# A fused attention and two-MLP kernel: values of two units issued from SP, zero matmuls in TensorE's pauses, and a new order

## The chip, the cores and the metric

The kernel runs on one core of a Trainium2 chip. The metric is the device time of one execution in microseconds. The core has five instruction streams: TensorE (PE, with its weight loads PEld), VectorE (DVE), ScalarE (ACT), GpSimd (POOL) and SyncE (SP), which here only issues DMAs. ACT issues a few DMAs too, at the start.

## The reference

Three stages follow each other, all in float32.

```python
# attention: 4 batches, 8 heads, 768 positions, 64 wide, 8 memory positions
for c in range(768 // 32):                       # chunks of 32 queries
    # keys and values: 8 memory rows, 16 to the left, the chunk, 8 to the right
    scores = (q_c @ k_full.T) / 8
    a = exp(scores - max(scores)); a = a / (sum(a) + 1e-9)
    out[c] = a @ v_full
x = out as 3072 tokens x 512
# first MLP
h = x @ w_in                                     # 512 -> 2048
P = a0 + a1*h + a2*h**2 + a3*h**3
Q = 1 + |b0|*|h| + |b1|*h**2
x = (P / (Q + 1e-6)) @ w_out                     # 2048 -> 512
# second MLP
y = (((x @ w1) * (x @ w2)) @ w3) @ w_out2        # 512 -> 1024, 1024 -> 512
```

## The kernel before

Attention goes in 24 units of 128 queries (two blocks of 64, all 8 heads). A unit is loaded as one tile of queries and keys (`qk`, 640 KB, L329, two buffers) and three pieces of values (L348: 64, 56 and 8 partitions, 524 KB together). `s_pe` (L370) makes its scores with 64 small matmuls; DVE and ACT do the softmax (L378 to L408: maximum, subtraction, exponent, sum, epsilon, reciprocal, scaling); `t_pe` (L413) transposes the weights into PSUM, `t_copy` (L421) copies them into `aT`, `v_pe` (L428) multiplies by the values, and `v_parts` (L436, L438) splits the result into a high and a low part. Every product that follows is made of three matmuls on such pairs (high by high, high by low, low by high; `mm3`, L317).

Three units make a block of 384 tokens, 8 blocks in all. For each of them and each of 16 slices of the 2048 hidden columns there is a first-layer product (`gemm1`, 36 matmuls in three groups for the first three slices, 12 each; tile `h`), a rational function over it that runs through ACT, POOL and DVE (L453 to L503, tiles `W`, `Q`, `A`, then `gh` and `gl`), and a second-layer product (`gemm2`, 12 matmuls on the four accumulators `acc`). The first eight slices of blocks 0 and 1 come first (`SEG`), so that the weights needed early are few. The second MLP follows with its own products (`ab`, `w3o`, `pr`).

The weights come as 64-bit floats of 512 KB a chunk (L270) into a ring of four raw buffers. `decode` turns a chunk into a high and a low part: ACT scales the upper words (L275), ACT or DVE takes the low bits (L281, L283), DVE joins them in two steps (L288, L290), ACT rounds the high part (L298), and POOL or DVE makes the low part (L301). A raw buffer is free again when the last of these has read it. Sixteen chunks (eight of `w_in`, eight of `w_out`) are needed for the first eight slices.

Every step is an object with a wanted time `t`, engines with costs, steps that it comes after, and ring slots that it takes. `order()` (L137) goes through them as a list scheduler and gives each engine its order; the table `SHIFT` moves single wanted times. The program's order on each engine is then fixed: an instruction waits for what it needs, and all behind it on its engine wait too. DMAs take one of eight completion semaphores in turn, whichever engine issues them, and a DMA waits until the earlier one on its semaphore has landed.

At the start, `start()` clears `aT` on POOL, loads the coefficients and an identity from ACT, and calls `load_v` for the three units of block 0. Those nine DMAs are issued by ACT, all others by SP:

```python
(act if u < UPB else sp).dma_start(out=t[r0:r1], ...)
```

The values of unit 0 lie in a raw buffer, those of unit 1 in the tile `x2_t` (named `x_t` in rows), those of unit 2 and all later ones in the one value buffer.

Of the kernel before, what the change touches and what calls it, by code (L numbers as in the profile page):

```python
# [7 lines left out]
F32 = mybir.dt.float32  # L8
# [8 lines left out]
P = 128  # L17
# [7 lines left out]
NS = 2  # L25
# [12 lines left out]
UPB = N // UQ  # L38
# [20 lines left out]
def attention_rational_mlp_gated_mlp(  # L59
# [33 lines left out]
    x2n = []  # L93

# [42 lines left out]
    def order():  # L137
        LOOK = 0.000
        warm = [0.0]
        todo, held, free, done = {}, {r: {} if rings[r] < 0 else [] for r in rings}, {"dma": 1.9, "act": 2.0}, []  # L140
# [52 lines left out]
        while len(done) < len(steps):  # L193
# [18 lines left out]
            if e == "pe":  # L212
                gap = s - free.get(e, 0.0)
                if gap > (4.0 if warm[0] >= 5.0 else 0.3):
                    warm[0] = 0.0
                if warm[0] < 5.0:
                    slow = min(2 * c, 5.0 - warm[0]) if c > 1 else 2 * c
                    warm[0] += slow if c > 1 else 0.0
                    c += slow / 2
# [117 lines left out]
    def load_v(u):  # L337
        b, j = divmod(u, UPS)
        if u == 0:
            t = raw32("v").rearrange("p (s h d) -> p s h d", s=NS, h=H)  # L340
        elif u == 1:
            t = x2_t.rearrange("p a c n -> p (a c n)")[:, :NS * H * D].rearrange("p (s h d) -> p s h d", s=NS, h=H)
        else:
            t = v_t[u % VBUF]
        vt[u] = t
        for r0, r1, k0 in ((0, CK, 0), (CK, P - NMEM, W1), (P - NMEM, P, 0)):
            if r1 < P or j < VBUF or u < UPB:
                (act if u < UPB else sp).dma_start(out=t[r0:r1], in_=vW[b, j * NS:(j + 1) * NS, k0:k0 + r1 - r0].rearrange("s k h d -> k s h d"))  # L348
# [280 lines left out]
    H0 = -3.298  # L629


    MODES = "nHhhkhNNnNNNHMNHnNhMMmHnnHNNhnMH"
# [4 lines left out]
    def start():  # L637
        pool.memset(aT, 0.0)
        act.preload_act_table_set("natural_log_exp_and_others")
        act.dma_start(out=cf, in_=coef)  # L640
        act.dma_start(out=idn, in_=ident)
        act.activation(out=cf[:, 4:6], in_=cf[:, 4:6], func=AF.Abs)
        act.activation(out=cf[:, 0:4], in_=cf[:, 0:4], func=AF.Copy, scale=-1.0)
        slots[:] = [("raw", 0)]
        for u in range(UPB):
            load_v(u)
# [4 lines left out]
    T0 = -2.290; UP = 0.175; A0 = -1.147; AS = 2.865  # L651
# [7 lines left out]

    SOFT = 3 * UPB  # L660
    VLAND = (7.6, 9.6, 11.6)
    LEAD = 15
    LEAD2 = 4
    A1 = -3.238
    A2 = -11.920

    def loads(u, t):
        lq[u] = step(t - 3, {"dma": 2.4 if u < 2 else 1.95}, lambda: load_qk(u), *old(first, lq[u - 1]), take=("q",))
        vm = u <= UPB or u % UPS < VBUF
        lv[u] = step(t - 2, {"none": VLAND[u]} if u < UPB else {"dma": 2.3}, lambda: u < UPB or load_v(u), *old(first, lv[u - 1] if u >= UPB else None), take=("raw",) if u == 0 else ("x2", "x2") if u == 1 else ("v",))  # L670
# [18 lines left out]
    def attend(u):  # L689
# [4 lines left out]
        tag1, tag2, tag3 = (("acc0", "acc1")[u % 2], ("h", "acc2")[u % 2], "acc3") if blk == 0 else TAGS1 if blk == 1 else ("h",) * 3  # L694
# [20 lines left out]
    R = (2.092,1.123,-0.489,1.317,7.957,11.098,8.651,1.756,-1.609,1.055,0.592,-0.348,-3.832,0.495)  # L715
    DI = 2.568
    DO = -1.081
    WI, WO = {}, {}
    SI = 0.414
    SO = 1.306  # L720
    DJ = -0.936
    DP = -3.866
    SJ = 0.526
# [45 lines left out]
    u = UPB  # L769
# [389 lines left out]
    for x, n in late:  # L1159
        x.after.append(G1[n])  # L1160
    SHIFT = {0: -8, 1: -23.66, 2: 1.74, 3: -13.58, 4: -13.83, 5: -46, 6: -23.07, 7: 3.51, 8: -44.34, 9: -49.07, 10: -32.57,
# [175 lines left out]
```

## Time and profile before

| | us |
|---|---|
| median of 3 runs (1071.61 to 1075.4) | 1072.48 |
| profiled execution | 1071.7 |
| its span, first to last instruction | 1069.9 |
| PE busy | 1034.6 (97%) |
| PEld busy | 982.5 (92%) |
| DVE busy | 737.6 (69%) |
| ACT busy | 664.1 (62%) |
| POOL busy | 505.7 (47%) |

The busy shares are means over the whole span. PE's is near full in all but the first two and the last of the page's 40 slices, while those of DVE, ACT and POOL fall from the first half to the second. The 1.8 us between the span and the profiled execution's time are start and end of the execution. The chain that ended last names PE for 80% of the span, ACT for 8%, DMA for 5%.

### The profile page before, as it was taken

The page shows a single profiled execution, that of the slowest core. Times are in us where ns is not written, and L with a number is a line of the kernel's source. Part 1 is how long each engine was busy: PE and PEld are TensorE (multiplying, and loading weights), DVE is VectorE, ACT ScalarE, POOL GpSimd, SP SyncE. Part 2 cuts the span into 40 slices and gives each one's busy share as a digit, 9 for nine tenths or more (in the row PEclk, how much of TensorE's full clock was granted, in tenths as well). Part 3 has the DMA queues.
Part 4 walks back from the last instruction along what each step waited for, and adds up shares of the span by engine and source line. Part 5 has one row for each costly group of instructions (what it writes and reads, how often), then busy time and mean ns, then how long its engine had stood idle before and what let it go on. Part 6 is the DMA issues. An engine that isn't in the chain of part 4 may idle for free.

```text
span 1069.9 us, 19764 instructions
## 1 busy us (share of the span) xinstructions
PE 1034.6 (97%) x7632; PEld 982.5 (92%) x7632; DVE 737.6 (69%) x1300; ACT 664.1 (62%) x1272; POOL 505.7 (47%) x490
## 2 busy tenths in 40 slices
PE   2699999999999999999999999999999999999998
PEld 2689999999999999999999999988899999998997
DVE  3899999877877767777778887678474653652330
ACT  2798998877676767767768996644342352342222
POOL 1464577644344544444455666543033362344233
PEclk9999999999999999999999999999999999999999
DMA  8755432123411211211131335544523122312101
GB/s 231 253 166 162 140 124 79 57 72 103 118 44 44 74 44 46 74 43 44 49 99 60 119 99 169 164 143 155 177 99 119 53 77 70 111 51 73 66 17 59
DMA packets 59613, 105.61 MB, mean 99 GB/s; under 512 B 4384, under 2 KB 29088, under 8 KB 59520
## 3 DMA queue, kind: packets, MB, share of 16 engines
q1 hardware_dynamic: 58350, 102.71, 30.6%
q10 hardware_dynamic: 1170, 1.64, 0.7%
q8 instruction: 60, 0.98, 0.4%
q14 instruction: 33, 0.27, 0.1%
HBM read 85.99 MB, written 18.35 MB: 98 GB/s over the span
## 4 chain that ended last, share of the span: by engine, by line
PE 80%; ACT 8%; DMA 5%; DVE 3%; issue 2%; POOL 1%; SPq 0%; ACTq 0%; POOLq 0%; DVEq 0%
PE acc L317 32%; PE h L317 21%; PE pr L317 16%; PE w3o L317 4%; PE xo L428 2%; PE sc L370 2%; PE ab L317 1%; ACT Q L462 1%; DMA w<-in_w_out_dram 1%; DMA qk<-in_qkT_dram 1%; DMA w<-in_w_in_dram 1%; ACT A L453 1%; PE at L413 1%; ACT W L453 1%; DMA w<-in_w_dram 1%
## 5 line engine op out<-in xcount | busy, mean ns | idle before, releaser
L317 PE MATMUL acc<-gh,wB 128*128 128x384 f32 x1024 | 283.7, 340 | 0.4 <-POOL wB L301 0.4
L317 PE MATMUL h<-xr,wA 128*128 128x384 f32 x1344 | 253.8, 338 | 0.6 <-DVE A L494 0.6
L317 PEld LDWEIGHTS h<-xr,wA 128*128 128x128 f32 x1344 | 234.9, 189 | 2.6 <-issue 0.8
L468 POOL TENSOR_TENSOR W<-W,Q 128x384 f32<-128x384 f32 x128 | 132.3, 1033 | 122.7 <-ACT Q L462 120.1
L317 PEld LDWEIGHTS acc<-gh,wB 128*128 128x128 f32 x1024 | 186.7, 188 | 2.4 <-POOL wB L301 0.7
L317 PE MATMUL acc<-gl,wB 128*128 128x384 f32 x512 | 172.3, 337 | 0.5 <-POOL gl L503 0.5
L503 POOL TENSOR_TENSOR gl<-A,gh 128x384 fp32r<-128x384 f32 x128 | 132.1, 1032 | 49.9 <-ACT gh L498 42.2
L486 DVE SCALAR_TENSOR_TENSOR A<-A,cf,h 128x384 f32<-128x384 f32 x128 | 78.1, 610 | 58.3 <-ACT h L482 57.8
L317 PE MATMUL pr<-wB,wA 128*128 128x384 f32 x624 | 113.7, 335 | 0.0
L317 PEld LDWEIGHTS pr<-wB,wA 128*128 128x128 f32 x624 | 109.2, 188 | 1.3
L473 DVE TENSOR_TENSOR A<-A,h 128x384 f32<-128x384 f32 x128 | 70.6, 552 | 43.2 <-ACT A L453 40.1
L317 PEld LDWEIGHTS acc<-gl,wB 128*128 128x128 f32 x512 | 96.1, 188 | 0.8 <-POOL gl L503 0.8
L317 PE MATMUL acc<-wB,gh 128*128 128x512 f32 x294 | 92.4, 395 | 0.0
L453 ACT ACTIVATE W<-h 128x384 f32<-128x384 f32 x128 | 62.3, 486 | 47.9 <-PE h L317 47.0
L462 ACT ACTIVATE Q<-W,cf 128x384 f32<-128x384 f32 x118 | 83.7, 709 | 3.8
L453 ACT ACTIVATE A<-h,cf 128x384 f32<-128x384 f32 x128 | 84.3, 658 | 1.3 <-PE h L317 1.1
L995 POOL TENSOR_TENSOR A<-A,Q 128x384 f32<-128x384 f32 x24 | 25.6, 1066 | 119.9 <-DVE A L995 119.9
L475 DVE SCALAR_TENSOR_TENSOR A<-A,cf,h 128x384 f32<-128x384 f32 x128 | 78.1, 610 | 2.3
L480 ACT ACTIVATE Q<-W 128x384 f32<-128x384 f32 x128 | 66.7, 521 | 16.3 <-POOL W L468 15.6
L995 DVE TENSOR_TENSOR A<-pr,W 128x384 f32<-128x384 f32 x48 | 26.7, 557 | 69.7 <-PE pr L317 69.4
L482 ACT ACTIVATE h<-Q 128x384 f32<-128x384 f32 x128 | 62.9, 492 | 16.6 <-DVE A L475 14.9
L494 DVE SCALAR_TENSOR_TENSOR A<-h,A 128x384 f32<-128x384 f32 x128 | 70.8, 553 | 2.2
(129 smaller groups left out, 1829.7 us busy)
## 6 DMA issues: line engine op xcount, KB each, us to landing
qk<-in_qkT_dram SPq DMA_DIRECT2D x24, 640.0 KB
w<-in_w_out_dram SPq DMA_DIRECT2D x24, 512.0 KB
sr<-sd SPq DMA_DIRECT2D x48, 256.0 KB
w<-in_w_in_dram SPq DMA_DIRECT2D x16, 512.0 KB
w<-in_w3T_dram SPq DMA_DIRECT2D x16, 512.0 KB
w<-in_w_dram SPq DMA_DIRECT2D x16, 512.0 KB
x2d<-x_t SPq DMA_DIRECT2D x16, 384.0 KB
out_dram<-oo SPq DMA_DIRECT2D x24, 256.0 KB
```

Source lines behind the costliest of these rows:

```text
L317: pe.matmul(out_, lhsT=wi(w, a), rhs=xi(x, c), start=first and i == 0, stop=last and i == 2, skip_group_check=more)
L453: act.activation(out=t, in_=hps[n][src], func=func, scale=scale, bias=bias)
L462: act.activation(out=t, in_=hps[n]["W"], func=AF.Identity, scale=cf[:, 5:6], bias=cf[:, 4:5])
L468: pool.tensor_tensor(out=W, in0=W, in1=Q, op=ALU.mult)
L473: dve.tensor_tensor(out=A, in0=A, in1=h, op=ALU.mult)
L475: dve.scalar_tensor_tensor(out=A, in0=A, scalar=cf[:, 1:2], in1=h, op0=ALU.add, op1=ALU.mult)
L480: act.activation(out=Q, in_=W, func=AF.Ln, bias=ONE)
L482: act.activation(out=h, in_=Q, func=AF.Exp, scale=-1.0)
L486: dve.scalar_tensor_tensor(out=A, in0=A, scalar=cf[:, 0:1], in1=r, op0=ALU.add, op1=ALU.mult)
L494: dve.scalar_tensor_tensor(out=A, in0=r, scalar=-2.0, in1=A, op0=ALU.add, op1=ALU.mult)
L503: eng.tensor_tensor(out=gl, in0=hps.pop(n)["A"], in1=gt[n].bitcast(F32), op=ALU.subtract)
L995: eng.tensor_tensor(out=t, in0=get(a), in1=get(b), op=ALU.add)
```

## The change

ACT issues the three value DMAs of unit 0 alone; those of units 1 and 2 are issued by SP, as steps that the scheduler places (before, the scheduler knew only the times at which they were expected to land, `VLAND`). A tile `zero` of 128x128 float32 is cleared by POOL ahead of `aT`. The function `awake` issues matmuls of this tile with itself into the bank of accumulator 2, which stands idle up to the first second-layer product; for this, the odd units of block 0 transpose into a bank `h` as the even ones do, no longer into that of accumulator 2. After each PE step ahead of the first second-layer product, `awake` is called with the number of zero matmuls that fill 0.75 of the pause which the scheduler expects there, at 0.125 us each (0.15 at the very start), less 0.4 us. There are 99 of them. The scheduler no longer models a slow TensorE after pauses. `MODES`, which says how each weight chunk is decoded, the wanted times of the rational's steps and of the chunks, and the table `SHIFT` have new values. What is computed stays as it was.

```diff
+    zero = const.tile([P, P], F32, name="zero")
+    idle_bank = []
+
+    def awake(n):
+        for _ in range(n):
+            pe.matmul(idle_bank[0][:, :P], lhsT=zero, rhs=zero, start=True, stop=True)
...
-                (act if u < UPB else sp).dma_start(out=t[r0:r1], in_=vW[b, ...
+                (sp if u else act).dma_start(out=t[r0:r1], in_=vW[b, ...
...
-    MODES = "nHhhkhNNnNNNHMNHnNhMMmHnnHNNhnMH"
+    MODES = "nHhhkhNNhNNkHNHNnNhMmhHHnkMhmMNn"
...
     def start():
+        pool.memset(zero, 0.0)
         pool.memset(aT, 0.0)
+        idle_bank.append(bank("acc2", "idle"))
...
-        for u in range(UPB):
-            load_v(u)
+        load_v(0)
...
-    T0 = -2.290; UP = 0.175; A0 = -1.147; AS = 2.865
+    T0 = -4.134; UP = -5.922; A0 = -0.586; AS = 2.299
...
+    FILL = 0.75
-    VLAND = (7.6, 9.6, 11.6)
-    LEAD = 15
-    LEAD2 = 4
+    LEAD = 14
+    LEAD2 = 2
...
-        tag1, tag2, tag3 = (("acc0", "acc1")[u % 2], ("h", "acc2")[u % 2], "acc3") if blk == 0 else ...
+        tag1, tag2, tag3 = (("acc0", "acc1")[u % 2], "h", "acc3") if blk == 0 else ...
...
-    SHIFT = {0: -8, 1: -23.66, 2: 1.74, 3: -13.58, 4: -13.83, 5: -46, 6: -23.07, 7: 3.51, ...
+    SHIFT = {0: 6.54, 1: -2.96, 2: -4.08, 3: -2.55, 4: 5.93, 5: 1.32, 6: -13.69, 7: -14.21, ...
...
     with tc.manual_schedule():
+        rest = {}
+        work = [x for x in done if x.eng == "pe"]
+        for x, y in zip([first] + work, work):
+            if y.start < G2[0].start:
+                rest[x] = int(FILL * max(0.0, y.start - max(x.end, 1.2) - 0.4) / (0.15 if x is first else 0.125))
         for x in done:
             slots[:] = x.slots
             x.f(...)
+            awake(rest.get(x, 0))
```

What moves is seen in the order of the instructions on the engines. In the rows, `qk` are queries and keys, `w` a raw weight chunk, `v` and `x_t` values, `sc` scores, `at` transposed weights of the softmax, `xo` the result of a unit, `h` a first-layer product. Lines of the kernel after are by two or three lower than before.

SP, the first entries of its queue before:

```order
L329 DMA qk_81<-in_qkT_dram 128x8x160
L270 DMA w_108<-in_w_in_dram 128x1024
L270 DMA w_110<-in_w_in_dram 128x1024
L329 DMA qk_82<-in_qkT_dram 128x8x160
L329 DMA qk_81<-in_qkT_dram 128x8x160
L270 DMA w_161<-in_w_in_dram 128x1024
L270 DMA w_207<-in_w_out_dram 128x1024
L329 DMA qk_82<-in_qkT_dram 128x8x160
L329 DMA qk_81<-in_qkT_dram 128x8x160
L270 DMA w_272<-in_w_in_dram 128x1024
L270 DMA w_300<-in_w_in_dram 128x1024
```

and now:

```order
L326 DMA qk_82<-in_qkT_dram 128x8x160
L326 DMA qk_83<-in_qkT_dram 128x8x160
L326 DMA qk_82<-in_qkT_dram 128x8x160
L345 DMA x_t<-in_vW_dram 64x2x512
L345 DMA x_t<-in_vW_dram 56x2x512
L345 DMA x_t<-in_vW_dram 8x2x512
L345 DMA v_84<-in_vW_dram 64x2x512
L345 DMA v_84<-in_vW_dram 56x2x512
L345 DMA v_84<-in_vW_dram 8x2x512
L326 DMA qk_83<-in_qkT_dram 128x8x160
L326 DMA qk_82<-in_qkT_dram 128x8x160
L267 DMA w_334<-in_w_in_dram 128x1024
```

Before, two weight chunks stood between the queries of units 0 and 1, and a chunk or two ahead of each further unit. Now the queries of units 0 to 4 and the values of units 1 and 2 stand ahead of the first chunk, and the next two entries of a unit (values of unit 3) follow four chunks later.

ACT, from the coefficients to its first work on a unit and on a weight, before:

```order
L348 DMA v<-in_vW_dram 64x2x512
L348 DMA v<-in_vW_dram 56x2x512
L348 DMA v<-in_vW_dram 8x2x512
L348 DMA x_t<-in_vW_dram 64x2x512
L348 DMA x_t<-in_vW_dram 56x2x512
L348 DMA x_t<-in_vW_dram 8x2x512
L348 DMA v_83<-in_vW_dram 64x2x512
L348 DMA v_83<-in_vW_dram 56x2x512
L348 DMA v_83<-in_vW_dram 8x2x512
L275 ACTIVATE w_108<-w_108 128x512
L275 ACTIVATE wx<-w_110 128x512
L390 ACTIVATE sc<-sc 128x512
```

and now:

```order
L641 ACTIVATE cf<-cf 128x2
L642 ACTIVATE cf<-cf 128x4
L345 DMA v<-in_vW_dram 64x2x512
L345 DMA v<-in_vW_dram 56x2x512
L345 DMA v<-in_vW_dram 8x2x512
L387 ACTIVATE sc<-sc 128x512 x2
L418 COPY aT<-at 64x16x32 x2
L396 ACTIVATE r<-sm 128x8
L387 ACTIVATE sc<-sc 128x512
```

Six DMAs and the first two weight steps are gone from the place ahead of the exponents; ACT's first step on a weight now stands behind the copies of the third unit.

PE, from its first instruction to the first first-layer product, before:

```order
L370 MATMUL sc<-qk_81 32x64 x32
L370 MATMUL sc<-qk_82 32x64 x32
L370 MATMUL sc<-qk_81 32x64 x32
L413 MATMUL at<-idn,e_84 128x128 x4
L428 MATMUL xo<-aT,v 64x64 x16
L413 MATMUL at<-idn,x_t 128x128 x4
L428 MATMUL xo<-aT,x_t 64x64 x16
L413 MATMUL at<-idn,e_84 128x128 x4
L428 MATMUL xo<-aT,v_83 64x64 x16
L370 MATMUL sc<-qk_82 32x64 x32
L317 MATMUL h<-xr,wA 128x384 x36
```

and now:

```order
L99 MATMUL idle<-zero 128x128 x24
L367 MATMUL sc<-qk_82 32x64 x32
L99 MATMUL idle<-zero 128x128 x14
L367 MATMUL sc<-qk_83 32x64 x32
L367 MATMUL sc<-qk_82 32x64 x32
L410 MATMUL at<-idn,e_85 128x128 x4
L99 MATMUL idle<-zero 128x128 x8
L425 MATMUL xo<-aT,v 64x64 x16
L410 MATMUL at<-idn,x_t 128x128 x4
L99 MATMUL idle<-zero 128x128 x8
L425 MATMUL xo<-aT,x_t 64x64 x16
L410 MATMUL at<-idn,e_85 128x128 x4
```

The useful steps stand in the same order; zero matmuls stand ahead of unit 0's scores, between them and unit 1's, and behind each transpose. Further groups of 8, 9, 12, 2 and 14 follow up to unit 3's values; where before three first-layer products stood in a row, unit 3's transposes and values now stand between them.

## Rows read from the trace of the kernel before

**Rows 1.** Windows: start:end, length, PE busy (instructions), granted clock, DMA share, GB/s.
```profile
0.00:55.40 55.40, 27.14 (x500) 1.00 0.82 241
55.40:100.00 44.60, 41.71 (x493) 1.00 0.59 171
100.00:1062.00 962.00, 961.40 (x6631) 1.00 0.28 87
...
0.00:17.00 17.00, 2.46 (x72) 1.00 0.94 243
```

**Rows 2.** Timeline, PE, 0 to 60: start, us, engine, line, operation, [idle before <-releaser].
```profile
5.87 2.02 PE L370 MATMUL sc<-qk 64*32 64x64 f32 x64 [5.87 <-DMA qk<-in_qkT_dram]
...
20.51 1.72 PE L370 MATMUL sc<-qk 64*32 64x64 f32 x56 [5.22 <-ACT qk L333]
...
24.81 1.11 PE L413 MATMUL at<-idn,e 128*128 128x128 f32 x4
27.80 1.97 PE L428 MATMUL xo<-aT,v 128*64 128x64 f32 x32 [1.87 <-ACT aT L421]
...
41.44 1.93 PE L370 MATMUL sc<-qk 64*32 64x64 f32 x64
43.31 7.58 PE L317 MATMUL h<-xr,wA 128*128 128x384 f32 x36
50.72 0.60 PE L413 MATMUL at<-idn,e 128*128 128x128 f32 x4
...
53.08 1.15 PE L428 MATMUL xo<-aT,v 128*64 128x64 f32 x32 [1.76 <-ACT aT L421]
54.39 1.10 PE L370 MATMUL sc<-qk 64*32 64x64 f32 x64 [0.16 <-DVE A L494]
55.42 0.44 PE L317 MATMUL acc<-gh,wB 128*128 128x384 f32 x1
```

**Rows 3.** Timeline, the DMA queues of ScalarE and SP, and ScalarE's first weight.
```profile
6.17 4.33 ACTq L348 DMA_DIRECT2D x_t<-in_vW_dram  x3
14.82 1.59 ACTq L348 DMA_DIRECT2D v<-in_vW_dram  x3
16.47 0.65 ACT L275 ACTIVATE w<-w 128x512 f32<-128x512 f32 x1 [13.61 <-DMA v<-in_vW_dram]
...
25.57 9.09 SPq L270 DMA_DIRECT2D w<-in_w_in_dram  x4
```

**Rows 4.** DMA packets of 9 to 12 us and of 27 to 30 us.
```profile
DMA packets 820, 0.69 MB, mean 229 GB/s; under 512 B 28, under 2 KB 693, under 8 KB 820
...
DMA packets 1287, 1.07 MB, mean 355 GB/s; under 512 B 32, under 2 KB 1211, under 8 KB 1287
```

**Rows 5.** DVE's windows (columns as above), the eighth rational's end, low part, PE.
```profile
core 0: us, DVE busy (x), PEclk, DMA share, GB/s
0.00:54.40 54.40, 33.95 (x61) 1.00 0.82 240
54.40:93.80 39.40, 37.08 (x68) 1.00 0.55 158
...
93.20 0.56 DVE L494 SCALAR_TENSOR_TENSOR A<-h,A 128x384 f32<-128x384 f32 x1
...
95.61 1.02 POOL L503 TENSOR_TENSOR gl<-A,gh 128x384 fp32r<-128x384 f32 x1
...
99.34 0.34 PE L317 MATMUL acc<-gl,wB 128*128 128x384 f32 x1
```

**Rows 6.** Timeline, ScalarE and POOL: copies, first product taken up, low parts.
```profile
32.84 1.17 ACT L421 COPY aT<-at 64x512 f32<-64x512 f32 x2
46.76 0.49 ACT L453 ACTIVATE W<-h 128x384 f32<-128x384 f32 x1 [0.69 <-PE h L317]
...
5.88 0.24 POOL L333 COPY qk<-qk 128x64 f32<-128x64 f32 x1 [4.20 <-DMA qk<-in_qkT_dram]
44.78 1.30 POOL L301 TENSOR_TENSOR wA<-w,wA 128x512 fp32r<-128x512 f32 x1 [1.93 <-ACT wA L298]
55.34 1.00 POOL L503 TENSOR_TENSOR gl<-A,gh 128x384 fp32r<-128x384 f32 x1
```

More of the change, by code (lines that the diff above doesn't have):

```diff
@@ L138, in order @@
         LOOK = 0.000
-        warm = [0.0]
-        todo, held, free, done = {}, {r: {} if rings[r] < 0 else [] for r in rings}, {"dma": 1.9, "act": 2.0}, []
+        todo, held, free, done = {}, {r: {} if rings[r] < 0 else [] for r in rings}, {"dma": 1.9, "act": 6.2}, []
         left = {x: len(x.after) for x in steps}
@@ L211, in order @@
             c = x.engines[e]
[L212 to L219, printed above, removed]
             x.eng, x.start, x.end = e, s, s + c
@@ L347, in load_v @@
             if r1 < P or j < VBUF or u < UPB:
-                (act if u < UPB else sp).dma_start(out=t[r0:r1], in_=vW[b, j * NS:(j + 1) * NS, k0:k0 + r1 - r0].rearrange("s k h d -> k s h d"))
+                (sp if u else act).dma_start(out=t[r0:r1], in_=vW[b, j * NS:(j + 1) * NS, k0:k0 + r1 - r0].rearrange("s k h d -> k s h d"))
     lent = wB[:, LENT:].rearrange("p f a k -> p (f a k)").rearrange("p (a c n) -> p a c n", a=2, c=KC)
@@ L628, in attention_rational_mlp_gated_mlp @@
     LOWA, PAIR, GLO, XLO = two('p', 1.36, .64), two('p', .551, .27), two('p', 1.04, .469), two('d', 1.764, .87)
-    H0 = -3.298
-    MODES = "nHhhkhNNnNNNHMNHnNhMMmHnnHNNhnMH"
+    H0 = -4.218
+    MODES = "nHhhkhNNhNNkHNHNnNhMmhHHnkMhmMNn"
     HOW = {"n": (None, LOWA), "h": ("h", LOWA), "m": (None, two("d", 0, .602)), "k": ("h", two("d", 0, .64))}
@@ L658, in attention_rational_mlp_gated_mlp @@
     tcs = {}
+    FILL = 0.75
     SOFT = 3 * UPB
-    VLAND = (7.6, 9.6, 11.6)
-    LEAD = 15
-    LEAD2 = 4
-    A1 = -3.238
-    A2 = -11.920
+    LEAD = 14
+    LEAD2 = 2
+    A1 = -4.172
+    A2 = -2.456
     def loads(u, t):
-        lq[u] = step(t - 3, {"dma": 2.4 if u < 2 else 1.95}, lambda: load_qk(u), *old(first, lq[u - 1]), take=("q",))
+        lq[u] = step(t - 3, {"dma": 2.4 if u < 2 else 1.95}, lambda: load_qk(u), *old(first, lq[u - 1], lv[0] if u == 1 else None), take=("q",))
         vm = u <= UPB or u % UPS < VBUF
-        lv[u] = step(t - 2, {"none": VLAND[u]} if u < UPB else {"dma": 2.3}, lambda: u < UPB or load_v(u), *old(first, lv[u - 1] if u >= UPB else None), take=("raw",) if u == 0 else ("x2", "x2") if u == 1 else ("v",))
+        lv[u] = step(t - 2 if u else -60, {"dma": 2.3 if u else 1.5}, lambda: u == 0 or load_v(u), *old(first, lv[u - 1] if u else lq[0]), take=("raw",) if u == 0 else ("x2", "x2") if u == 1 else ("v",))
         return lq[u]
@@ L693, in attend @@
         sk = loads(u, t)
-        tag1, tag2, tag3 = (("acc0", "acc1")[u % 2], ("h", "acc2")[u % 2], "acc3") if blk == 0 else TAGS1 if blk == 1 else ("h",) * 3
+        tag1, tag2, tag3 = (("acc0", "acc1")[u % 2], "h", "acc3") if blk == 0 else TAGS1 if blk == 1 else ("h",) * 3
         if u % UPS < QBUF:
@@ L712, in attend @@
         outs(u, t + 1.3 * k, k)
-    R = (2.092,1.123,-0.489,1.317,7.957,11.098,8.651,1.756,-1.609,1.055,0.592,-0.348,-3.832,0.495)
-    DI = 2.568
-    DO = -1.081
+    R = (-2.991,1.867,-0.232,1.904,8.471,4.955,7.110,2.056,-4.730,0.267,-1.467,-1.098,-3.807,-0.335)
+    DI = 2.107
+    DO = -1.960
     WI, WO = {}, {}
[L719 to L723, printed above, removed]
+    SI = 0.473
+    SO = 1.225
+    DJ = 0.295
+    DP = -1.364
+    SJ = 0.215
     chunks = sorted([(SI * f + DI if f < HF else SJ * (USE[f] - USE[HF]) + DJ + USE[HF], 0, f) for f in range(NF1)]
@@ L1160, in attention_rational_mlp_gated_mlp @@
         x.after.append(G1[n])
-    SHIFT = {0: -8, 1: -23.66, 2: 1.74, 3: -13.58, 4: -13.83, 5: -46, 6: -23.07, 7: 3.51, 8: -44.34, 9: -49.07, 10: -32.57,
[107 rows of a table removed]
+    SHIFT = {0: 6.54, 1: -2.96, 2: -4.08, 3: -2.55, 4: 5.93, 5: 1.32, 6: -13.69, 7: -14.21, 8: 4.3, 9: 2.4, 10: 6.84, 11:
[104 rows of a table added]
     for i, d in SHIFT.items():
```

211 rows, old and new, of the table SHIFT are left out of this document.

## The prediction

> **What bounds the kernel now.** I read the windows of PE first. From 100 to 1062 us PE is busy 961.40 of 962 us [rows 1], so the steady part has nothing left to win there, and all that a new order can move lies in the first 100 us: PE is busy only 27.14 of the first 55.4 us and 41.71 of the next 44.6 [rows 1]. That is 28.3 + 2.9 = 31.2 us of idle time. The timeline of PE says what the 28 us are [rows 2]: the scores of unit 0 at 5.87, most of unit 1's only from 20.51 (5.22 us of the wait are for ScalarE's copy of an operand), then a slow alternation of transposes and value products up to the first-layer product at 43.31, and the first second-layer product at 55.42. From there on PE has hardly any idle time.
>
> Second, the queues [rows 3]. ScalarE issues three DMAs of unit 1's values from 6.17 and three of unit 2's from 14.82, and starts its first activation on a weight only at 16.47. Between 10.5 and 14.8 it sits in a queue entry that waits for unit 1's queries and keys, and everything behind that entry (the decode of the weights, the copy that unit 1's scores need) waits too. Third, DVE: 33.95 us of work in the first 54.4 us, nearly nothing before 17, then 37.08 of 39.4 us up to the end of the eighth rational at 93.8 [rows 5]. DVE is the second bound of the start.
>
> A fourth thing hides in durations. The granted clock reads 1.00 in every stretch, but the same 64 score matmuls take 1.93 us at 41.44 and 1.10 at 54.39, four transposes 1.11 and 0.60, a value product 1.97 and 1.15 [rows 2]: up to the first products PE works at the lower of its two levels (1.2 GHz), after them at 2.4. The level rose inside the 36 products at 43.31 (7.58 us), after PE had been busy without a pause for the scores before them.
>
> **The change, part by part.** *Queues.* SP now issues query/key loads of units 0 to 4 and the values of units 1 and 2 ahead of any weight; ScalarE issues three DMAs and is free. Unit 1's queries land behind unit 0's alone instead of behind two weight chunks. Unit 0's scores still start near 5.87. The bytes ahead of the end of unit 1's load are 0.66 + 0.66 MB, with up to 0.52 MB of values alongside, against 3.5 MB that were moved by 14.8; at 229 to 355 GB/s [rows 4] the second 0.66 MB takes 1.9 to 2.9 us, so it lands at 7.8 to 8.8. Gain at this link: 6 to 7 us, and the 5.22 us until 20.51 [rows 2] disappear, since POOL now copies that operand, in 0.24 us as it did for unit 0 [rows 6].
>
> *Weights move back.* Ahead of the first chunk's end lie five query/key loads, three value loads and itself: 3.28 + 1.57 + 0.52 = 5.4 MB. The windows give 243 GB/s over the first 17 us, 4.1 MB [rows 1]; at 229 to 355 [rows 4] the other 1.3 MB takes 3.7 to 5.7 us, so it lands at 20.7 to 22.7; I take 21.5. Each further chunk (0.52 MB) takes 1.5 to 2.3 us.
>
> *The attention chain.* Unit 0's scores are done at 7.9 as before. DVE's steps at 0.6 (its mean is 37.08/68 = 0.55 with short ones among them [rows 5]) and the exponent at 0.59 (half of 1.17 [rows 6]) end at about 11.7; unit 2's queries land near 12.2, its scores end at 13.3. Then transpose 0.60, two copies on ScalarE 1.17 [rows 6], value product 1.15, three times, with hand-overs: 3.0 us per unit, so 22.3. Unit 3's scores end at 23.4. The first chunk needs scale, three joins, high part and POOL's low part of 1.30 [rows 6] and is ready at 25.9; the first product runs to 28 (before: 46.7, where ScalarE takes it up at 46.76 [rows 6]). The chain behind a product, from there to POOL's low part at 55.34 + 1.00 [rows 6], is 9.6 us. The next two products wait for their chunks (ready at 30.6 and about 33), and unit 3's values and unit 4's scores stand ahead of the second-layer product too: second product 30.6 to 32.8, 14 zeros and unit 3's values to 36.1, third product to 38.3, scores to 39.4. So it starts at 39.4 against 55.42. PE has done the same useful work by then in both orders, so **by PE's account the gain is 16.0 us**.
>
> *DVE gives part of it back.* Before, 27 decode steps were done on DVE ahead of the first rational's end, now 16; up to the eighth end the counts are level (128 instructions before, 131 now, three more at about 0.6). So DVE must do 71.03 + 1.7 = 72.7 us up to that point. Before, it idled 22.8 of the 93.8 us. Now it idles 7.9 us up front, about 5 us in the chain (0.65 for an exponent, 0.65 for unit 2's scores, 1.75 between two low parts, 1.2 on the first chunk, small ones), and 2.3 us later as in [rows 5]. Sum 72.7 + 15.2 = 87.9 against 93.8: 5.9 us earlier. PE took the eighth pair up 2.7 us after it was ready (96.63 to 99.34 [rows 5]), so PE can be 8.6 us earlier without waiting. That is the lower end, 16.0 the upper; I take 9.5, near the lower, since DVE was at 94% in that stretch.
>
> *Zero matmuls.* 99 of them, each 0.28 (1.11/4) at the lower level or 0.15 at the upper [rows 2]: 14.9 to 27.5 us of PE, all ahead of 39 us. The 24 at the start run from about 1.2 and end at 4.8 to 7.9; unit 0's scores end at 7.9 either way (5.87 + 2.02 slow, or 6.8 + 1.10). The 14 behind them (2.1) end before unit 1's softmax can use its scores (DVE is free at 11.7). Each 8 (1.2) lie beside the two copies of 1.17. The 9 and 12 lie beside the decode of the first two chunks. The 14 ahead of unit 3's values cost up to 0.7. At the upper level their net cost is near nothing; what they buy is the excess of the lower level, 0.83 + 0.51 + 0.82 per unit in a chain that is now serial.
>
> *The rest of the new order.* PE's spare is 0.6 us of 962 [rows 1], so it can't gain there. It can lose: in PE's order at least 5.5 blocks of 12 matmuls now lie between a product and its second layer from the eighth on, 6.3 before. At 7.58 / 3 = 2.5 us a block [rows 2] (partly at the lower level) that is 13.9 against 15.9 us, and the chain is 9.6. I count nothing and keep 2 us for the range.
>
> **Sum.** 1071.7 - 9.5 = 1062.2; the median of the runs stands 0.8 above the profiled execution, so 1063.0. About 0.5% (5.4 us) is what a measurement can tell from no change.
>
> **Rivals.** *The level stays low (chance 0.16).* Scores, transposes and value products from 20.51 to 41.44 left the level low [rows 2]; the fill covers three quarters of the planned pauses and may not do either. Then two scores, three transposes and three value products cost 1.66 + 1.53 + 2.46 more, the three sets of 8 zeros outlast the copies by 1.05 each, the 9 by 1.15, the first product 1.3: 11.2 us. Second layer at 50.6, gain 4.8: 1067.7. Against it: PE will be busy almost without a pause from 1.2 us.
>
> *The queue swap saves issue time only (0.10).* Six DMAs leave ScalarE, at 0.53 us each (1.59/3 [rows 3]), 3.2 us; if the loads are a matter of bytes and DVE fills its idle time no better, the time is 1072.5 - 3.2 = 1069.3. The Trainium skill (DMA: Bandwidth & Descriptors, Issuing engines are not separate DMA queues) says just that: loads issued from several engines share the same DMA engines, and a second issuer saves only the issuing time. By that rule the sum would be this rival's. The trace differs at this place: ScalarE lost 13.6 us in front of its first weight [rows 3], a wait inside the queue and not the issuing.
>
> *The first weights come too late (0.07): slower.* DVE then has nothing to decode after unit 2. Every us that the first chunk lands after 21.5 is a us of DVE idle, which uses up the gain at 31 and costs over 0.5% from about 36.4 us on; at 40 it is 9.0 us slower, 1081.5. For it: four raw buffers in a ring, whose four refills took 9.09 us at 25.57 [rows 3], and value loads that wait for a value product now stand ahead of weights on SP. Against it: 36 us would mean 150 GB/s, and no saturated row is below 229.
>
> Something in between, no measurable change, gets 0.07; the forecast 0.60, its own range 1057 to 1067 (gains of 15.5 to 5.5).
>
> **How the numbers follow.** Faster by over 0.5% is below 1067.1: 0.57 of the forecast's 0.60, 0.08 of the low level's 0.16, 0.03 of the issue-time rival: 0.68. Slower 0.07, the rest 0.25. The range 1057 to 1071.5 leaves out the late weights, some of the in-between case and the last of the forecast's best.
>
> **What would show it.** Right: unit 1's scores by 9.6, ScalarE at softmax work by 9, the first product near 26, the second layer near 39, scores at 1.10 from unit 1 on, and PE idle again for some us between 40 and 85 with DVE above 95%. Wrong: scores at 1.9 after 10 us; a first weight landing after 25; or PE without idle time from 39 on, which would make the gain 16.

## The result: 0.55% slower, and the profile after

| | before | after |
|---|---|---|
| median (6 runs each, same chip), us | 1072.76 | 1078.4 |
| profiled execution, us | 1071.7 | 1078.66 |
| its span, us | 1069.9 | 1076.9 |
| mean granted clock of TensorE | 1.000 | 0.994 |

The ratio is 1.0055 (95% interval 1.0043 to 1.0067). The forecast was 1063.0, with 1071.5 as its upper end. (Of the kernels below, e7 was profiled in a slow execution, 1145.6 us at a granted clock of 0.849, so its places are not used.)

The start did become faster. PE's timeline up to the first second-layer product (columns as in [rows 2]):

```profile
0.99 7.66 PE L99 MATMUL idle<-zero 128*128 128x128 f32 x48 [0.99 <-POOL zero L635]
8.58 1.10 PE L367 MATMUL sc<-qk 64*32 64x64 f32 x64
9.61 3.39 PE L99 MATMUL idle<-zero 128*128 128x128 f32 x28
12.93 1.10 PE L367 MATMUL sc<-qk 64*32 64x64 f32 x64
...
18.16 1.15 PE L425 MATMUL xo<-aT,v 128*64 128x64 f32 x32
...
31.24 2.35 PE L314 MATMUL h<-xr,wA 128*128 128x384 f32 x12 [0.56 <-DVE w L287]
...
46.82 0.44 PE L314 MATMUL acc<-gh,wB 128*128 128x384 f32 x1
```

The first hidden product starts at 31.24 instead of 43.31, the first second-layer product at 46.82 instead of 55.42 [rows 2]. Scores take 1.10 us from unit 0 on: the level is high early. The first 24 zero matmuls (48 records, two for each call) end at 8.65, though, and unit 0's scores start 2.7 us later than before.

That is a lead of 8.6 us at the first second-layer product. PE's windows, as [rows 1], show where it went:

```profile
0.00:46.80 46.80, 43.63 (x698) 1.00 0.85 240
46.80:100.00 53.20, 44.28 (x480) 0.87 0.58 175
100.00:1062.00 962.00, 958.31 (x6616) 1.00 0.28 88
```

From 46.8 to 100 us PE idles 8.9 us, against 2.9 in the corresponding stretch before, and the granted clock, 1.00 there before, is 0.87. From 100 to 1062 it idles 3.7 us instead of 0.6. From the first second-layer product to the end both kernels run the same number of PE records, first before, then after:

```profile
55.40:1069.90 1014.50, 1007.51 (x7140) 1.00 0.29 91
46.80:1076.90 1030.10, 1013.64 (x7140) 0.99 0.29 92
```

The change loses 15.6 us there, 7.0 more than its lead: 9.5 us of it is more idle time (16.5 against 7.0), and for 6.1 us the same instructions take longer. The stretch from 53 us on, from PE's timeline:

```profile
53.23 0.63 PE L410 MATMUL at<-idn,e 128*128 128x128 f32 x4
55.88 3.72 PE L314 MATMUL h<-xr,wA 128*128 128x384 f32 x12 [2.02 <-ACT aT L418]
59.53 1.30 PE L425 MATMUL xo<-aT,v 128*64 128x64 f32 x32
60.76 1.10 PE L367 MATMUL sc<-qk 64*32 64x64 f32 x64
...
67.65 0.63 PE L410 MATMUL at<-idn,e 128*128 128x128 f32 x4 [1.37 <-DVE e L405]
68.03 2.40 PE L314 MATMUL h<-xr,wA 128*128 128x384 f32 x12
73.71 1.97 PE L425 MATMUL xo<-aT,v 128*64 128x64 f32 x32 [3.28 <-ACT Q L477]
77.81 1.93 PE L367 MATMUL sc<-qk 64*32 64x64 f32 x64 [2.13 <-DVE A L491]
79.67 4.21 PE L314 MATMUL h<-xr,wA 128*128 128x384 f32 x12
```

Four pauses of 2.02, 1.37, 3.28 and 2.13 us, and behind three of them work at the lower level: a product in 3.72 or 4.21 us that takes 2.3 elsewhere, scores in 1.93. The last step of the eighth rational, 93.20 before [rows 5], is at 95.78; that of the first came 12.0 us earlier than before (41.78 against 53.78). The chain of waits says what stands behind the longest pause (start, us, what; some pieces left out):

```profile
55.88 3.72 PE h L314 x12
59.60 1.26 PE xo L425 x32
...
60.87 0.63 SPq L345
...
62.23 6.47 DMA qk<-in_qkT_dram
...
68.72 0.24 ACT qk L330
68.96 0.40 ACT W L450
...
69.39 0.71 ACT Q L459
70.10 0.56 ACT A L450
...
71.65 0.59 ACT aT L418
```

Unit 4's value product frees the one value buffer; only then does SP issue unit 5's values, and behind them unit 7's queries, which take 6.47 us to land. ACT stands at the copy of their memory keys, with the `W`, `Q` and `A` of a finished hidden product behind it. The scores that need this copy run at 93.76.

### The profile page after: what moved, and what is told of

It is laid out like the page before. It is cut to its first block, busy times and chain, and to the rows that moved or that the text cites. A ratio compares the mean times of both kernels' runs of the same rounds, so it can differ in the third digit from the quotient of the medians.

```text
span 1076.9 us, 20193 instructions
## 1 busy us (share of the span) xinstructions
PE 1057.3 (98%) x7830; PEld 1004.8 (93%) x7830; DVE 732.6 (68%) x1300; ACT 664.2 (62%) x1270; POOL 505.4 (47%) x493
## 4 chain that ended last, share of the span: by engine, by line
PE 80%; ACT 7%; DMA 7%; POOL 2%; issue 2%; DVE 2%; SPq 0%; POOLq 0%; ACTq 0%
PE acc L314 32%; PE h L314 21%; PE pr L314 16%; PE w3o L314 4%; DMA w<-in_w_in_dram 3%; DMA w<-in_w_out_dram 2%; PE sc L367 2%; PE ab L314 2%; PE xo L425 2%; DMA qk<-in_qkT_dram 1%; ACT Q L459 1%; POOL wA L298 1%; PE idle L99 1%; ACT A L450 1%; PE at L410 1%
## 5 line engine op out<-in xcount | busy, mean ns | idle before, releaser
L470 DVE TENSOR_TENSOR A<-A,h 128x384 f32<-128x384 f32 x128 | 70.4, 551 | 39.1 <-ACT A L450 36.2
L477 ACT ACTIVATE Q<-W 128x384 f32<-128x384 f32 x128 | 67.0, 523 | 17.4 <-POOL W L465 16.5
```

Of the source, the lines that this page charges most:

```text
L470: dve.tensor_tensor(out=A, in0=A, in1=h, op=ALU.mult)
L477: act.activation(out=Q, in_=W, func=AF.Ln, bias=ONE)
```

## The experiments

Each kernel is one edit of the changed kernel or of the kernel before. The results together; "late idle" is PE's idle time from 100 to 1062 us in the profiled execution, and "early" is span less late idle, less the same for before (1069.9 - 0.6 = 1069.3). The executions behind one ratio lie 2.4 to 7.9 us apart: e1's profiled one stands 2.8 us above its median, e3's 2.8 below. Their starts differ too: the first second-layer product is at 46.82 in the change and, with the same steps up to there, at 50.59 in e6. So these two columns show places, and the ratio tells faster from slower.

| run | ratio to before (95%) | span | late idle | early |
|---|---|---|---|---|
| the change | 1.0055 (1.0043 to 1.0067) | 1076.9 | 3.7 | +3.9 |
| e1 no zero matmuls | 1.0035 (1.0017 to 1.0052) | 1076.5 | 3.1 | +4.1 |
| e2 values back on ACT | 1.0059 (1.0033 to 1.0084) | 1079.9 | 4.6 | +6.0 |
| e3 new order alone | 1.0082 (1.0056 to 1.0108) | 1076.6 | 2.5 | +4.8 |
| e4 old order, values on SP | 0.9979 (0.9963 to 0.9996) | 1066.8 | 0.0 | -2.5 |
| e5 first chunks ahead | 1.0057 (1.0039 to 1.0075) | 1078.9 | 4.7 | +4.9 |
| e6 fill carried on | 1.0067 (1.0046 to 1.0088) | 1077.5 | 4.6 | +3.6 |
| e7 as e4, with zeros | 0.9992 (0.9982 to 1.0002) | | | |
| e8 one copy to POOL | 1.0047 (1.0026 to 1.0068) | 1078.4 | 5.8 | +3.3 |
| e9 two copies late | 1.0050 (1.0035 to 1.0065) | 1074.4 | 4.4 | +0.7 |
| e10 as e9, with zeros | 1.0032 (1.0020 to 1.0044) | 1074.1 | 5.0 | -0.2 |
| e11 as e4, third chunk ahead | 0.9988 (0.9974 to 1.0002) | 1067.6 | 0.3 | -2.0 |
| e12 as e10, a chunk's steps late | 1.0034 (1.0021 to 1.0046) | 1072.7 | 4.8 | -1.4 |

### Which of the three parts: e1 to e4

e1, the changed kernel without `awake`:

```diff
-            awake(rest.get(x, 0))
```

> The changed kernel without its zero matmuls; order, queues and everything else as in it. In the changed kernel the 24 zero matmuls at the start ended 2.7 us after unit 0's queries had landed, and after the last zeros (44 us) TensorE paused 2.0, 1.4, 3.3 and 2.1 us between 53 and 78 us, with products at 3.7 to 4.3 us behind the pauses instead of 2.1. Theory F (the fill is too long and costs its 2.7 us): unit 0's scores start at 5.9 again and the end comes 2 to 3 us earlier, 1075.5. Theory C (the clock level is what matters): early scores, value products and the first hidden products take twice as long (1.9 to 2.0 and 3.8 to 4.2 us), the first second-layer product comes at 48 to 52 instead of 46.8, and the end 0 to 5 us later, 1078 to 1083. Theory O (the new order holds the work up between 50 and 100 us whatever the start does): the end within 1 us of 1078.4.

e2, in the changed kernel the three units' values issued by ACT in `start()`:

```diff
-        load_v(0)
+        for u in range(UPB):
+            load_v(u)
...
-                (sp if u else act).dma_start(out=t[r0:r1], ...
+                (act if u < UPB else sp).dma_start(out=t[r0:r1], ...
```

> The changed kernel with the values of units 1 and 2 issued by ScalarE at the start again, as before; zero matmuls and order stay. Theory Q (the six value pieces and the two query loads that stand on SyncE ahead of the first weights cost the start): the first weight is issued at about 12.5 instead of 16.5 and lands near 22 instead of 26.1, the first second-layer product comes 3 to 4 us earlier, and the end 3 to 4 us earlier, 1074 to 1075.5. Theory O (the new order loses the lead between 50 and 100 us anyway): the weight may land earlier, but the end stays within 1 us of 1078.4.

e3 has both edits.

> Both of these undone: the new order of steps alone, without zero matmuls and with the three units' values on ScalarE. Theory O: 1077 to 1080, no zero matmul and no queue is needed for the loss. Theories Q and F together: about 1072.5, as the kernel before. Theory C: low level at the start as before, 1076 to 1082.

e4 is the kernel before, with units 1 and 2's values on SP behind unit 2's queries:

```diff
-        for u in range(UPB):
-            load_v(u)
+        load_v(0)
...
+            if x is lq[2]:
+                load_v(1)
+                load_v(2)
```

> The kernel before with one part of the change alone: the values of units 1 and 2 are issued by SyncE behind the third unit's queries, not by ScalarE. Theory Q: the weights behind them come 3 to 4 us later than before and so does the end, 1075 to 1077. Theory O: the start of the old order has slack, 1072 to 1073.5.

The new order alone (e3) is slower by 0.56 to 1.08%, so it needs neither zeros nor queues to be slow. That is theory O in kind, though 1.0082 is 8.8 us, above its range and inside theory C's. e3 still holds the change's new decode table (`MODES`) and unit 1's transposes in another bank. The transposes ran without a wait before them (at 25.39 in e3, 19.25 in the change); the table is not separated from the order of the steps by any run.

e1 bears out half of two theories. Without zeros, scores took 2.02 us again, unit 0's started at 5.82, and the first second-layer product came at 49.14, 2.3 us later than in the change (theory C), though the first hidden product, at 31.37, did not. The ratio is 0.20% below the change's, 2.1 us, as theory F said; but the two intervals overlap, so what the zeros cost at the end is not shown. In e2 the end is hardly later (theory O), and the first hidden product comes at 35.91, which theory Q expected earlier: SP issued the first chunk at 21.46 there, at 16.53 in the change.

e3 and e1 differ by the queue of the values alone, and their intervals do not touch: in the new order without zeros, issuing them from SP is worth 0.47%. With zeros (e2 and the change) no such gain is seen.

e4 went against both theories: in the old order the first part of the change is a gain, 0.04 to 0.37%. ACT's first scalings of weight chunks in e4:

```profile
7.27 0.69 ACT L275 ACTIVATE w<-w 128x512 f32<-128x512 f32 x1 [4.58 <-DMA w<-in_w_in_dram]
10.10 0.66 ACT L275 ACTIVATE wx<-w 128x512 f32<-128x512 f32 x1 [2.14 <-DMA w<-in_w_in_dram]
...
23.75 0.62 ACT L275 ACTIVATE wx<-w 128x512 f32<-128x512 f32 x1 [8.70 <-DMA w<-in_w_in_dram]
```

The first is at 7.27 instead of 16.47 [rows 3]; then ACT waits 8.7 us for the third chunk, and the first rational's last step comes 2.0 us earlier (51.83 against 53.78).

### What eats the lead: e5, e6, e8

e5 moves three weight loads on SP, e6 adds zeros on an accumulator behind four steps, e8 gives one copy to POOL:

```diff
+        ahead = [steps[i] for i in (51, 58, 72)]          # e5
+        done = [x for x in done if x not in ahead]
+        k = done.index(lq[2]) + 1
+        done[k:k] = ahead
...
+        more = {steps[316]: 8, steps[432]: 5, steps[447]: 13, steps[380]: 8}      # e6
+            for _ in range(more.get(x, 0)):
+                pe.matmul(accs[0][2][:, :P], lhsT=zero, rhs=zero, start=False, stop=False, ...)
...
+        steps[402].eng = "pool"          # e8
```

> The changed kernel with the first three weight chunks moved, in SyncE's order, from behind the values of units 1 and 2 and the queries of units 3 and 4 to right behind unit 2's queries; all other orders stay. Theory W (the chunks come too late and their decoding, not the first product, sets the pace: the first eight chunks are decoded by 59.4 us here, by 46.1 before): the first chunk lands by 20 instead of 26.1, unit 0's first hidden product starts by 27 instead of 31.2, the eighth hidden product by 75 instead of 79.7, and the end comes 3 to 5 us earlier, about 1074. Theory O (the later places of the order hold it up whatever the first chunks do): an earlier first product, the eighth hidden product within 1 us of 79.7, the end within 1 us of 1078.4. Against both: the values of units 1 and 2 land some 4 us later, and if units 1 and 2 were short of them the end would be 1 to 3 us later.

> The changed kernel with its fill carried on: 34 more zero matmuls, which add zero to an accumulator of the second layer, in the four longest pauses between 53 and 78 us (8, 5, 13 and 8 of them at 0.24 us each, sized by the pauses of 2.0, 1.4, 3.3 and 2.1 us). Theory C (the level that falls in these pauses costs the lead): the products behind them take 2.1 to 2.3 us instead of 3.7 to 4.2, the value product and the scores 1.1 instead of 1.9 to 2.0; that is about 5 us of TensorE, and the end comes 3 to 5 us earlier, 1073.5 to 1075.5. Theory O or W (TensorE waits there for other engines): the products are short, but the pauses grow by as much, and the end is within 1 us of 1078.4.

> The changed kernel with one copy moved: the memory keys of unit 7, for which ScalarE waited 1.76 us until 68.72 us with the sixth hidden product's first reading and its slope behind it, go to GpSimd. If ScalarE's wait for that load is what keeps the fifth value product until 73.7 us: that product 1.5 to 2 us earlier, end 1 to 2 us earlier. If not (decoding sets the pace): the same end within 0.7 us.

e5: ACT no longer waited for the first chunks, but unit 1's value product now waited 2.94 us for its values, and the first hidden product came at 33.82, later than in the change. Moving some bytes forward delayed others here. e6 did what theory C wanted and gained nothing at the end:

```profile
72.17 3.06 PE L1279 MATMUL acc<-zero 128*128 128x128 f32 x26
75.23 1.15 PE L425 MATMUL xo<-aT,v 128*64 128x64 f32 x32
76.31 2.05 PE L1279 MATMUL acc<-zero 128*128 128x128 f32 x16
79.37 1.10 PE L367 MATMUL sc<-qk 64*32 64x64 f32 x64 [1.01 <-DVE A L491]
80.40 2.35 PE L314 MATMUL h<-xr,wA 128*128 128x384 f32 x12
```

The work is at the upper level (1.15, 1.10 and 2.35 us), and the eighth hidden product stands at 80.40 all the same. The second layer began late in this execution, at 50.59; but e5, as late at 50.06 and without these zeros, has that product at 80.75. So PE waits for others there, and the interval, from 1.0046 on, excludes the 3 to 5 us of theory C. e8 only moved the wait. POOL now stands at the copy, with the low part of a weight chunk behind it (the second row below), and a hidden product waited 1.40 us for that. The profile puts POOL's 3.48 us down to transposes that had just ended, but what the copy reads is the load that SP issued at 64.05:

```profile
70.20 0.35 POOL L330 COPY qk<-qk 128x64 f32<-128x64 f32 x1 [3.48 <-PE at L410]
70.51 1.29 POOL L298 TENSOR_TENSOR wA<-w,wA 128x512 fp32r<-128x512 f32 x1
```

### The waits taken away: e9, e10, e12

e9 issues two copies of memory keys (units 6 and 7) later, both on POOL. e10 adds 26 zeros. e12 is e10 with three decode steps of a late chunk moved behind other work:

```diff
+        for i, j in ((385, 127), (402, 148)):          # e9, e10, e12
+            x = steps[i]
+            x.eng = "pool"
+            done.remove(x)
+            done.insert(done.index(steps[j]) + 1, x)
...
+        more = {steps[316]: 8, steps[432]: 5, steps[447]: 8, steps[380]: 5}          # e10, e12
...
+        for i, j in ((186, 577), (185, 577), (187, 595)):          # e12, moved likewise
```

> The changed kernel with two small copies issued later: the memory keys of units 6 and 7, which GpSimd and ScalarE copy (0.24 us each) as soon as those units' queries land, while the engine stands still for the load 3.0 and 1.8 us; both now stand on GpSimd some 10 to 15 us later, still ahead of the scores that read them. Theory S (in-order waits on a load that is not yet needed: value product 4, unit 5's values, unit 7's queries, that copy, then the sixth hidden product's chain): the fifth value product 2 to 3 us earlier than 73.7, the eighth hidden product 2 to 4 us earlier than 79.7, the end 2 to 4 us earlier, ratio 1.002 to 1.004. Theory D (decoding and DVE's work pace this stretch): the wait goes elsewhere, the eighth rational still ends at 95 to 98, ratio 1.0045 to 1.0065.

> The same with 26 zero matmuls added in the pauses between 53 and 78 us, on an accumulator, as in the earlier run with 34. Theory S with C: without the wait the products are on TensorE's path and the level counts: a further 1.5 to 3 us earlier, ratio 1.000 to 1.002. Theory D: as the run without zeros, within 1 us.

> The changed kernel with the late copies and the 26 added zero matmuls (which gave 1.0032), and one more in-order wait taken away: ScalarE stood from 113.0 to 114.7 us for a weight chunk issued at 108.2, with unit 8's two copies, W, Q and A of a hidden product behind it; the chunk's two ScalarE steps and its first join on DVE now stand behind those. Theory S (each lead is given back at the next engine that waits in order for a load; take the waits away one by one and the lead stays): TensorE's waits between 97 and 200 us, 3.1 us, fall to 1 to 1.5, and the ratio to 1.001 to 1.002. Theory D (DVE and the decoding set this stretch): the wait comes back at the next product, 1.003 to 1.004.

In e9 unit 5's value product is at 70.56 instead of 73.71 and the eighth hidden product at 77.41 instead of 79.67, as theory S said; the eighth rational ends at 93.0 instead of 96.3. The ratio stayed inside theory D's range; late idle was 4.4 us. e10 brings the eighth hidden product to 76.52, and its ratio lies between the ranges of both theories. Its interval, 1.0020 to 1.0044, reaches that of the change (from 1.0043) only at its edge: of the 0.55%, 0.23 are gone by the middle values. DVE's windows up to the end of the eighth rational, the change and then e10:

```profile
0.00:9.79 9.79, 0.00 (x0) 1.00 0.77 194
9.79:42.30 32.51, 24.81 (x48) 1.00 0.89 254
42.30:96.33 54.03, 45.63 (x86) 0.87 0.56 171
```

```profile
0.00:9.79 9.79, 0.00 (x0) 1.00 0.75 195
9.79:43.40 33.61, 24.87 (x48) 1.00 0.83 246
43.40:91.30 47.90, 45.26 (x85) 1.00 0.62 193
```

The work is the same (45.63 and 45.26 us in the third row); DVE's idle time beside it falls from 8.4 to 2.6 us. The same stretch in e9 (copies late, no added zeros), e6 (added zeros, copies in place) and e5 (neither):

```profile
42.65:92.97 50.32, 45.26 (x85) 0.93 0.59 183
46.10:95.72 49.62, 45.25 (x85) 1.00 0.61 190
45.56:96.95 51.39, 45.64 (x86) 0.90 0.59 181
```

e9 begins the stretch where the change does and leaves 5.1 us, so the copies alone took 3.3 away, and the zeros beside them another 2.4. e6 leaves 4.4, but it begins the stretch 3.8 us later, and e5, late as well, leaves 5.8 with neither. What is left of the loss in e10's profiled execution is the late idle, which PE's waits from 97 us on name in e10 (total us, times, longest):

```profile
PE h L314 <- DVE A L491: 3.1, 4, 1.4
PE ab L314 <- ACT W L584: 1.9, 1, 1.9
```

e12 cut the first to 2.3 us, while the second rose to 2.4; its ratio is e10's, as theory D said. All ten profiled kernels with the new order have 2.5 to 5.8 us of late idle, the three with the old order 0 to 0.6. That this belongs to the new order, with its decode table, is shown; which of its rows would have to move was not found.

### Can the old order take more: e7, e11

e7 adds 83 zero matmuls to e4, after the steps that end ahead of its own pauses; e11 puts the third chunk's load ahead of the values:

```diff
+        rest = {first: 13, steps[4]: 18, steps[21]: 7, steps[12]: 22, steps[29]: 8, steps[45]: 9, steps[300]: 6}   # e7
...
-            if x is lq[2]:          # e11, against e4
+            if x is steps[58]:
```

> The kernel before with the values of units 1 and 2 on SyncE (which alone gave a ratio of 0.9979) and 83 zero matmuls in the pauses up to the first second-layer product, sized by its own pauses at 0.24 to 0.32 us each. If a high level pays in the old order: early scores and value products 1.1 us instead of 2.0, the first second-layer product at about 52 instead of 54, the end 1 to 2 us earlier than without zeros, ratio 0.9960 to 0.9970. If the early part waits for DVE and ScalarE anyway: ratio 0.9975 to 0.9985. If the zeros stand in the way of late steps: over 1.

> The kernel before with the values of units 1 and 2 on SyncE, and the third weight chunk's load ahead of them instead of behind (one load moved against the run that gave 0.9979). There, ScalarE and DVE stood still from 17.1 to 23.7 us for that chunk, issued at 14.28 and landed at 23.75. Theory L (late chunks set the old order's start): it lands by 17 to 19, the first hidden product starts 3 to 5 us earlier than 42.0, and the end comes 2 to 5 us earlier, ratio 0.993 to 0.996. If other loads or the ring of four raw buffers take its place: 0.997 to 0.999. If unit 1's or 2's values become late: 1.000 or more.

Neither improves on e4: 0.9992 (in none of the ranges named) and 0.9988. In e11 the chunk is taken up at 18.39, as theory L said, but the next one then waits:

```profile
18.39 0.62 ACT L275 ACTIVATE wx<-w 128x512 f32<-128x512 f32 x1 [3.22 <-DMA w<-in_w_in_dram]
...
25.74 0.62 ACT L275 ACTIVATE wx<-w 128x512 f32<-128x512 f32 x1 [5.67 <-DMA w<-in_w_out_dram]
```

The first hidden product starts at 42.07, in e4 at 42.04. e4 is the one version whose interval lies below 1, if only by 0.04%.

## Why the prediction was wrong

**What bounds the kernel: right.** The steady part had nothing to win, and the first 100 us were where the order could gain.

**Loads: the waits in SP's queue were left out.** ACT took the first chunk up at 26.07, forecast 21.5; unit 1's queries kept its scores until 10.58 in e1 (no zeros in front), forecast 7.8 to 8.8. The forecast let one load follow the other as before, 4.1 MB in 17 us. But there are two query buffers, and SP stands in its queue until scores free one: unit 2's load began at 9.79, behind unit 0's scores and so behind the zeros, and the first chunk's only at 16.53, behind unit 4's queries, which went out at 16.46, after unit 2's scores. PE's windows in the change, with GB/s last:

```profile
0.00:17.00 17.00, 15.27 (x279) 1.00 0.82 201
17.00:26.07 9.07, 9.07 (x146) 1.00 1.11 322
```

Up to 17 us the loads ran at 201 GB/s instead of 243 [rows 1]; the tail did run at the rate forecast, but by 26.07 it was 6.34 MB that had moved and not 5.4, for three more chunks were under way.

**Attention chain and PE's account: right in direction.** The second layer began at 46.82, forecast 39.4: a lead of 8.6 us, not 16.0.

**Zero matmuls: mis-sized.** A call costs 0.32 us at the start (7.66/24) and 0.24 later (3.39/14), not 0.28 and 0.15. The 24 at the start end at 8.65, forecast 4.8 to 7.9. That they raise the level was right; next to e1, which has none, no gain from it is seen at the end.

**DVE's account: the step that failed.** The forecast was 72.7 of work, and idle times of 7.9 up front, 5 in the chain and 2.3 later: 87.9. Measured: 70.4 of work, and 9.8, 7.7 and 8.4: 96.3. The term "2.3 us later as in [rows 5]" alone is 6.1 us off, of 8.4 in all. I took it over from the old order without asking what stands behind each wait in the new one. In the old order the copies of units 6 and 7 stood right behind their loads as well, but both on POOL:

```profile
62.54 0.24 POOL L333 COPY qk<-qk 128x64 f32<-128x64 f32 x1 [3.36 <-DMA qk<-in_qkT_dram]
74.35 0.24 POOL L333 COPY qk<-qk 128x64 f32<-128x64 f32 x1 [2.17 <-DMA qk<-in_qkT_dram]
```

POOL waited 3.4 and 2.2 us for them, and DVE idled 2.3 us all the same. In the new order one of the two is ACT's, with the chain of a finished product behind it, and PE's pauses bring the level down. With the two copies moved (e9) this term measures 5.1, with zeros in the pauses as well (e10) 2.6, and the eighth rational ends at 91.3. So the work was counted nearly rightly (2.3 us too high) and the waits were not. The Trainium skill (PSUM — Partial Sum Buffer, Engine vs sequencer instructions) says that the queues of ScalarE, VectorE and GpSimdE are strictly first in, first out; the trace agrees: the hidden product at 64.01 was done at 66.28, and its `W` stood behind the copy until 68.87.

**The rest of the new order: the second failure.** "I count nothing and keep 2 us for the range": late idle rose from 0.6 to 3.7 us. The count of blocks between a product and its second layer did not see it; the waits are for `A` and for `W`, not for second layers.

**Rivals.** The low level came true, but after 53 us instead of at the start, and was not the cause alone (e6). Late weights, at 0.07, had the right sign and named a load behind the value product. Its price of 1 us per us stays untested: in e5 the first chunk was issued 6 us earlier, at 10.46, but taken up later, at 27.89, behind unit 1's late values. The rival that the queue swap saves issue time only, 3.2 us, fits what e4 measures for that part alone: 0.21%, 2.3 us. The rule of the Trainium skill that was named with it (DMA: Bandwidth & Descriptors, Issuing engines are not separate DMA queues) thus agrees in size: though ACT's first weight came 9.2 us earlier, only about the issuing time was won. In the new order without zeros the same part was worth 5.0 us by the middle values (e3 to e1), more than the issuing. That the order itself could cost time with nothing else changed was none of my rivals; it stood only as 2 us in the range.

**The signs to look for.** A first weight after 25 was named as proof against the forecast, and it came at 26.07.

## What to carry to other kernels

A lead at the first product is worth only what the stage behind it can hold: here loads that waited for a buffer, and engines that stood in order for those loads, turned much of 8.6 us into pauses. Before you add up an engine's work and take its idle time from the old trace, go through the new order of every engine and ask at which instruction it will stand for a load, and what is behind it that could run; a copy of 0.24 us that was needed only 25 us later held up a whole chain here. When a change has parts, time each part alone, and beside the others: the one small part here was a gain that the order hid, larger beside the bare order than in the old one.

## What the runs showed of the hardware

A float32 matmul of 128x128 by 128x128 appears as two records. TensorE's level can fall after dense work: 3.72 us for 12 matmuls behind a pause of 2.02 us in the change and 3.11 behind one of 1.81 in e3, yet 2.35 behind one of 1.81 in e9. Zero matmuls keep it up (granted clock 1.00 from 46.8 to 100 us in e6, where the change has 0.87), and a matmul of zeros added to an open accumulator is a way to do so when no bank is free; by itself that gained nothing at the end here (e6), where other engines set the pace.
